# Transposing and loading DMAs taken out of each other's way, residual rows loaded earlier, and the static order of the engines planned anew, in a transformer block of attention and gMLP

## The chip, the cores and the metric

The kernel runs on one core of a Trainium2 chip. Times are device microseconds of that core. Engines: PE is TensorE (matmul), PEld its weight loads, DVE is VectorE, ACT is ScalarE, POOL is GpSimd, SP is SyncE. SP and POOL here mainly issue DMAs, each from one queue worked in order.

## The reference

```python
h  = x + A(layernorm(x))     # x: 2048 x 1024
h2 = h + B(layernorm(h))
# A: q,k,v = x@wqkv; 32 heads of 32; each row attends to 8 rows (0,2,..14 back); then @wo
# B: z = gelu(x@w_in); z1 = left half; z2 = layernorm(right half)
#    g = w_sp @ z2 + b_sp   (w_sp: 2048 x 2048);  return (z1*g) @ w_out
```

## The kernel before

The rows are worked in four chunks of 512. A first phase does q, k, v (`qkv`), attention on DVE, the projection with wo plus residual (`head`), and the two halves of w_in (`b_z2`, `b_z1`). A second phase multiplies by w_sp and w_out. In the first phase a small planner (`Order`) lists every piece of work with an estimated duration, and writes one fixed order for PE, ACT and DVE; engines then only wait on semaphores. DMAs are not in that fixed order.

```python
XRB = 2
o_ = Order({"PE": 22.2, "ACT": 23.3, "DVE": 17.0, "POOL": 17.0},
           {"acc": 3, "L": 1, "prod": 2, "part": 2, "xn": 4})    # start clocks, buffers
X_AT = {1: 18.8, 2: 33.0, 3: 38.0}                               # when x is expected
...
# ln1: four stores of normalised rows, then ONE transposing DMA per chunk
    nc.sync.dma_start_transpose(xnT[c][:], xn_d[c].rearrange("s (a p) -> s a p", p=P))
...
# head: residual rows x ("xr"): two loaded at the start, the others when a buffer is free
    for k in range(min(XRB, TPC)): xr_load(k)
    ...
    V.scalar_tensor_tensor(hb, acc, 1.0, st["xr", il][:], ...)   # h = acc + x
    A.activation(st["xr", il][:], hnc[:, il, :], ACTF.Square, ...)
    if il + XRB < TPC: xr_load(il + XRB)
...
def zload():                                                     # POOL queue, 12 loads
    for i in range((NCH - 1) * TPC):
        dma_w(z2sb[i][:], z2_d[i * P:(i + 1) * P, :])
def wsp0():                                                      # SP queue
    i_ = load_wsp(0)     # transposes 512 x 2048 of w_sp; only order-tied to a z1 store
...
dma_w(wout_a[:], wout_view[:, 0:8, :])                           # POOL queue
dma_w(wout_b[:], wout_view[:, 8:NF, :])
```

Three buffers called `acc` take PE's results. ACT empties them into four buffers (tag "xn"), which SP stores to memory. If SP can't issue a store, ACT soon can't empty, and PE stops.

Of the kernel before, what the change touches and what calls it, by code (L numbers as in the profile page):

```python
# [33 lines left out]
XRB = 2  # L34
# [23 lines left out]
class Order:  # L58

    def __init__(self, clocks, slots):  # L60
        self.ops, self.clock, self.slots, self.table = [], dict(clocks), {k: [0.0] * n for k, n in slots.items()}, None

# [9 lines left out]
    def run(self):  # L72
        left = list(self.ops)
        while left:
            best, cand = None, []
            for o in left:
                if any(d.end is None for d, _ in o.deps):
                    continue
                r = max([d.end + lat for d, lat in o.deps], default=0.0)
                short = False  # L80
                for k in o.take:
                    if self.slots[k]:
                        r = max(r, min(self.slots[k]))
                    else:
                        short = True
                if short:
                    continue
                cand.append((max(r, self.clock.get(o.eng, 0.0)), o))
            assert cand, "nothing can start"
            first = {}  # L90
            for t, o in cand:
                if o.eng not in first or t < first[o.eng]:
                    first[o.eng] = t
            eng = min(first, key=lambda e: first[e])
            mine = [(o.prio, t, o.n, o) for t, o in cand if o.eng == eng and t <= first[eng] + 0.02]
            late = [(o.prio, t, o.n, o) for t, o in cand if o.eng == eng and t > first[eng] + 0.02]
            pick = min(mine, key=lambda x: x[:3])
            for x in sorted(late):
                if x[0] < pick[0] - 0.5 and x[1] < pick[1] + (0.0 if eng == "PE" else 0.3) * pick[3].us:
                    pick = x  # L100
                    break
            _, t, _, o = pick
            if o.table and o.table != self.table:
                t += 1.28
                self.table = o.table
            o.start, o.end = t, t + o.us
            if o.eng in self.clock:
                self.clock[o.eng] = o.end
            for k in o.take:
                self.slots[k].remove(min(self.slots[k]))  # L110
            if o.free:
                self.slots[o.free].append(o.end + 0.1)
            left.remove(o)
        self.ops.sort(key=lambda o: (o.start, o.n))
        for o in self.ops:
            o.fn()

@with_exitstack
def kernel(
# [185 lines left out]
    o_ = Order({"PE": 22.2, "ACT": 23.3, "DVE": 17.0, "POOL": 17.0}, {"acc": 3, "L": 1, "prod": 2, "part": 2, "xn": 4})  # L305
# [6 lines left out]
    X_AT = {1: 18.8, 2: 33.0, 3: 38.0}  # L312
# [3 lines left out]
    def ln1(c):  # L316
# [16 lines left out]
        else:  # L333
# [11 lines left out]
            rs = batch_rstd(("l1", c), lambda: G["xsum", c][:], lambda: G["xsq", c][:], D, "l1", sts, 1.0)  # L345
# [7 lines left out]
        ns = [dma_op(4.0, lambda: None, [n_], free="xn") for n_ in ns]  # L353
        def tr():
            xnT[c] = xtp.tile([P, KT, CH], BF16, name="xnT", tag="xnT")
            nc.sync.dma_start_transpose(xnT[c][:], xn_d[c].rearrange("s (a p) -> s a p", p=P))
        G["xnT", c] = dma_op(8.0, tr, ns + ([G["qkvlast", c - 2]] if c >= 2 else []))
# [7 lines left out]
    def qkv(c):  # L365
        for xi in range(0 if c else 1, 3):
            wv = wsb[xi][:].rearrange("p kt (m dl) -> p kt dl m", dl=DLO)
            for dp in range(DLO // 2):
                key = ("acc", "qkv", c, xi, dp)
                deps = [G.get(("xnT", c))]  # L370
                for j, kh in ((0, 0), (0, 1), (1, 0), (1, 1)):
                    def mm(j=j, kh=kh, dl=2 * dp + j, wv=wv, key=key):
                        if j == 0 and kh == 0:
                            G[key] = new_acc()
                        for kt in range(4 * kh, 4 * kh + 4):
                            G["wdoneins", c] = T.matmul(G[key][:, j, :], wv[:, kt, dl, :], xnT[c][:, kt, :],  # L376
                                                        start=(kt == 0), stop=(kt == KT - 1))
# [19 lines left out]
    def attention(c):  # L397
# [3 lines left out]
        else:  # L401
            def ld(which):
                def f():
# [3 lines left out]
                    dma_w(att_in[c][which][:], qkv_d[which][:, :, lo:(c + 1) * CH])  # L407
                return f
            ev = [G["ev", c, xi, dp] for xi in range(3) for dp in range(4)]
            d_q = dma_op(7.0, ld(0), ev[0:4] + [G["qkdone", c - 1]])  # L410
# [76 lines left out]
        def rec():  # L487
            st["rinv"] = att.tile([P, P], FP32, name="rinv", tag="rinv")
# [4 lines left out]
        for hw in range(2):  # L493
# [7 lines left out]
            for sh in range(2):  # L501
# [10 lines left out]
                pm = add("PE", 0.2, pbm, [wait], prio=1.0, take="acc" if sh else "L", lat=0.2)  # L512
# [7 lines left out]
        for w in range(W_WIN):  # L520
# [15 lines left out]
            else:  # L536
                prev = add("DVE", 2.3, lambda w=w: V.tensor_tensor(oTs[c][:], oTs[c][:], pvs[w][:], op=ALU.add),  # L537
                           [prev, m_], prio=3.0, lat=0.15, free="prod")
        G["avdone", c] = prev

    def batch_rstd(key, sums, sqs, n, pfx, deps, prio, cols=slice(0, TPC), nb=True):
        def a1():
            if cols.start == 0:
# [7 lines left out]
        s2 = add("POOL", 1.05, lambda: nc.gpsimd.tensor_tensor(G[key]["rstd"][:, cols], G[key]["var"][:, cols], nhalf[:, cols], op=ALU.pow),  # L551
                 [s1], lat=POOLLAT)
# [5 lines left out]
    def head(c):  # L558
# [4 lines left out]
        xr0 = dma_op(0.0, lambda: None, [G["attq", c]] if ("attq", c) in G else [])  # L563
        sqd = []
        for il in range(TPC):
            i = c * TPC + il
            deps = [G["avdone", c]]
            for half in range(4):
                def mm(half=half, il=il, i=i):
                    if half == 0:  # L570
                        if il == 0:
# [3 lines left out]
                            for k in range(min(XRB, TPC)):  # L575
                                xr_load(k)
# [5 lines left out]
                def xr_load(k):  # L582
                    st["xr", k] = bp.tile([P, D], BF16, name="xr", tag="xr", bufs=XRB)
                    dma(st["xr", k][:], x2d[(c * TPC + k) * P:(c * TPC + k + 1) * P, :])
# [8 lines left out]
            def hsq(il=il):  # L593
                A.activation(st["xr", il][:], st["hnc"][:, il, :], ACTF.Square, accum_out=st["hsq"][:, il:il + 1])
                if il + XRB < TPC:
                    xr_load(il + XRB)
# [18 lines left out]
        if last:  # L615
            G["close"] = dma_op(0.0, close_, [G["headmm", c]] + [G["z2n", k, il] for k in range(c) for il in range(TPC)])
            tps = []
            for il in range(TPC):
# [6 lines left out]
                t_ = add("PE", 0.45, tpm, [nd[il]], prio=1.0, take="acc")  # L625
# [3 lines left out]
        else:  # L629
            def tr():  # L630
                hnTs[c] = bp.tile([P, TPC, KT, P], BF16, name="hnT", tag="hnT")
                nc.sync.dma_start_transpose(hnTs[c][:].rearrange("p il a s -> p (il a) s"),
                                            st["hnc"][:].rearrange("s il (a p) -> s (il a) p", p=P))
            G["hnT", c] = dma_op(8.0, tr, nd)
# [93 lines left out]

    def load_wo():
        i_ = dma_w(wo_sb[:], A_wo.rearrange("(p dl) n -> p dl n", dl=DLO))  # L730
        tc.add_manual_dep(i_.ins, G["wdoneins", 0].ins.name,
                          mybir.DependencyInfo(mybir.DependencyClass.Sync, mybir.DependencyReason.DATA),
                          reason="load wo behind the first chunk")

    dma_op(8.0, load_wo, [G["wdone", 0, 2]])
# [31 lines left out]
    def zload():  # L767
        for i in range((NCH - 1) * TPC):
            dma_w(z2sb[i][:], z2_d[i * P:(i + 1) * P, :])

    head(NCH - 1)
    dma_op(0.0, zload, [G["hdone", NCH - 1], G["close"]])
# [3 lines left out]
    def wsp0():  # L776
# [3 lines left out]
                          reason="keep the xbar transpose out of the z1 store stream")  # L780

    dma_op(0.0, wsp0, [G["z1ev", NCH - 2], G["close"]])
# [11 lines left out]
    dma_w(wout_a[:], wout_view[:, 0:8, :])  # L794
    dma_w(wout_b[:], wout_view[:, 8:NF, :])
    for c in range(NCH):
        wspT = wspTs[c]
        zg = p2.tile([P, NF, CH], BF16, name="zg", tag="zg")
        for fp in range(NF // 2):
# [3 lines left out]
            for j in range(2):  # L803
                f = 2 * fp + j
                for a in range(NT):
                    T.matmul(acc[:, j, :], z2sb[a][:, f * P:(f + 1) * P], wspT[:, a, :],  # L806
                             start=(a == 0), stop=(a == NT - 1))
# [48 lines left out]
```

## Time and profile before

| | before |
|---|---|
| median, first 4 runs | 733.63 us (732.98 to 734.22) |
| span of the profiled run | 731.48 us |
| PE busy | 720.2 us, 98% |
| first k matmul starts at / span after the last matmul | 23.96 us / 3.33 us |

The first two lines of the profile page of the kernel before, span and engine totals (busy us, share, number of instructions):

```profile
span 731.5 us, 8470 instructions
PE 720.2 (98%) x3453; PEld 365.1 (50%) x3514; DVE 418.1 (57%) x427; ACT 246.5 (34%) x313; POOL 46.8 (6%) x59
```

PE is the bound, and what can be won is its waits. The list of waits of PE in the kernel before (engine, tile, line, releaser: total us, times, longest):

```profile
PE wps L204 <- DVE warm L201: 1.3, 1, 1.3
PE L L453 <- DVE part L437: 1.1, 1, 1.1
PE tp L246 <- DVE xn L235: 0.8, 1, 0.8
PE acc L284 <- ACT xnT L249: 0.5, 1, 0.5
PE tpa L246 <- DVE xn L235: 0.4, 1, 0.4
PE tp L624 <- DVE hb L609: 0.3, 1, 0.3
```

Lines L204, L246 and L284 are the start-up. Only L453 (attention logits, waiting for DVE) and L624 (a transpose on PE, waiting for DVE) lie in the stream.

The list leaves waits out that end inside a matmul's modelled length. A finer reading of the trace compares starts of neighbouring matmuls, which are about 216 ns apart at 512 columns, and calls more than that a stall. One caution: about one matmul record in fifty is missing, and such a hole looks like a stall of 216 ns. The weight loads are recorded completely (3514), so a hole with two weight loads in it is a missing record, and a hole with one is a stall. Read that way, the kernel before has five stalls after 20 us: 0.22 us at 69.3, 0.24 at 214.4, 1.16 at 236.8, 0.23 at 384.4 and 0.47 at 391.8, together 2.32 us.

Why DVE was late at 237 shows in its timeline around the residual addition (start, duration, engine, line, operation, in brackets the idle time before it and what ended it):

```profile
209.53 2.29 DVE L430 TENSOR_TENSOR prod<-qT,kT 128x4096 bf16<-128x4096 bf16 x1
213.48 1.23 DVE L589 SCALAR_TENSOR_TENSOR hb<-acc,xr 128x1024 bf16<-128x1024 f32 x1 [1.67 <-DMA xr<-in_A_x_dram]
```

DVE stood 1.67 us waiting for rows of x that were loaded late, and everything behind it moved.

### The profile page before, as it was taken

The numbers are of one execution on the slowest core, as the hardware profiler recorded it, in microseconds if no ns is written. First come the engines' busy times: TensorE is split into PE (matmuls) and PEld (weight loads), VectorE is DVE, ScalarE is ACT, GpSimd is POOL, SyncE is SP. The second block draws the span as 40 slices with busy tenths as digits, with TensorE's granted clock in tenths as the row PEclk, the third lists the DMA queues.
The fourth block names the chain that finished last, engine by engine and source line by source line (L and its number), as shares of the span: only waits on it lengthen the run. The fifth ranks groups of instructions, "written<-read, shape, count | busy, mean of one in ns | idle before, by whom it ended". The sixth has DMA issues, their size and how long they took to land.

```text
span 731.5 us, 8470 instructions
## 1 busy us (share of the span) xinstructions
PE 720.2 (98%) x3453; PEld 365.1 (50%) x3514; DVE 418.1 (57%) x427; ACT 246.5 (34%) x313; POOL 46.8 (6%) x59
## 2 busy tenths in 40 slices
PE   8999999999999999999999999999999999999998
PEld 3666665666644444444445444444444444444444
DVE  5489999989989999989942102322232223222222
ACT  4396822543338954687634530000000000000000
POOL 0111200100101000100113100000000000000000
PEclk9999999999999999999999999999999999999999
DMA  8976874385682623360239997044115311020002
GB/s 322 353 169 217 229 233 146 119 243 187 215 305 73 231 86 103 102 216 15 108 136 343 248 243 244 30 121 124 58 33 126 116 58 42 25 91 16 1 16 71
DMA packets 113814, 106.30 MB, mean 145 GB/s; under 512 B 67856, under 2 KB 91824, under 8 KB 113648
## 3 DMA queue, kind: packets, MB, share of 16 engines
q1 hardware_dynamic: 105696, 72.82, 33.3%
q0 software_dynamic: 7280, 31.50, 12.7%
q10 hardware_dynamic: 800, 1.44, 0.5%
q8 instruction: 27, 0.44, 0.3%
q14 instruction: 11, 0.09, 0.0%
HBM read 55.09 MB, written 34.93 MB: 123 GB/s over the span
## 4 chain that ended last, share of the span: by engine, by line
PE 89%; DMA 5%; DVE 4%; issue 1%; ACT 1%; SPq 0%; DVEq 0%; ACTq 0%
PE acc L806 26%; PE acc L376 19%; PE acc L825 13%; PE acc L707 12%; PE acc L657 10%; PE acc L580 6%; DVE prod L430 2%; DMA qkv_d<-stg 1%; PE acc L284 1%; DMA xr<-in_A_x_dram 1%; DMA h_d<-hb 1%; DMA xp<-in_A_x_dram 1%; DVE prod L434 1%; DMA wq<-in_A_wqkv_dram 1%; DVE hb L589 1%
## 5 line engine op out<-in xcount | busy, mean ns | idle before, releaser
L806 PE MATMUL acc<-wspT,z2sb 128*128 128x512 bf16 x878 | 193.1, 379 | 0.9
L806 PEld LDWEIGHTS <-z2sb 128*128 128x128 bf16 x896 | 87.7, 98 | 105.7
L809 DVE TENSOR_TENSOR g<-acc,bB 128x1024 bf16<-128x1024 f32 x28 | 34.3, 1224 | 159.5 <-PE acc L806 134.3
L707 PE MATMUL acc<-hnT,win 128*128 128x512 bf16 x448 | 98.7, 379 | 0.1
L657 PE MATMUL acc<-win,hnT 128*128 128x512 bf16 (+1 forms) x500 | 98.0, 352 | 0.7
L430 DVE TENSOR_TENSOR prod<-qT,kT 128x4096 bf16<-128x4096 bf16 x32 | 72.5, 2283 | 8.6 <-DMA xp<-in_A_x_dram 8.6
L657 PEld LDWEIGHTS <-hnT 128*128 128x128 bf16 x512 | 49.8, 98 | 47.7 <-issue 1.1
L825 PEld LDWEIGHTS <-zg 128*128 128x128 bf16 x462 | 45.2, 98 | 51.7
L707 PEld LDWEIGHTS <-win 128*128 128x128 bf16 x448 | 43.4, 98 | 52.6 <-issue 1.9
L531 DVE TENSOR_TENSOR prod<-vT,AB 128x4096 bf16<-128x4096 bf16 x28 | 63.8, 2289 | 1.0
L537 DVE TENSOR_TENSOR oT<-oT,prod 128x4096 bf16<-128x4096 bf16 x28 | 64.0, 2285 | 0.1
L827 DVE TENSOR_TENSOR ot<-acc,hr 128x1024 bf16<-128x1024 f32 (+2 forms) x18 | 19.9, 1106 | 73.1 <-PE acc L825 64.2
L825 PE MATMUL acc<-wout_a,zg 128*128 128x512 bf16 (+1 forms) x260 | 58.0, 372 | 0.3
L376 PE MATMUL acc<-xnT,wk 128*128 128x512 bf16 x251 | 56.2, 379 | 0.3
L376 PE MATMUL acc<-xnT,wv 128*128 128x512 bf16 x250 | 56.1, 380 | 0.3
L580 PE MATMUL acc<-wo_sb,oT 128*128 128x512 bf16 x251 | 55.8, 379 | 0.3
L387 ACT CAST stg<-acc 128x1024 bf16<-128x1024 f32 x36 | 36.2, 1010 | 51.9 <-PE acc L376 42.5
L376 PEld LDWEIGHTS <-wk 128*128 128x128 bf16 x256 | 36.9, 145 | 18.9 <-issue 0.7
L376 PEld LDWEIGHTS <-wv 128*128 128x128 bf16 x256 | 36.7, 145 | 18.8 <-issue 0.9
L825 PE MATMUL acc<-wout_b,zg 128*128 128x512 bf16 (+1 forms) x193 | 43.8, 372 | 0.2
L376 PE MATMUL acc<-xnT,wq 128*128 128x512 bf16 x188 | 42.6, 380 | 0.2
L580 PEld LDWEIGHTS <-oT 128*128 128x128 bf16 x256 | 25.0, 98 | 29.7
(107 smaller groups left out, 525.1 us busy)
## 6 DMA issues: line engine op xcount, KB each, us to landing
qkv_d<-stg SPq DMA_DIRECT2D x36, 256.0 KB, 2.9
z_d<-z1s SPq DMA_DIRECT2D x28, 256.0 KB, 2.6
z1c<-z_d SPq DMA_DIRECT2D x28, 256.0 KB, 2.7
z_d<-u SPq DMA_DIRECT2D x12, 448.0 KB, 2.8
z2sb<-z_d POOLq DMA_DIRECT2D x12, 448.0 KB, 8.1
xr<-in_A_x_dram SPq DMA_DIRECT2D x16, 256.0 KB, 2.6
h_d<-hb SPq DMA_DIRECT2D x16, 256.0 KB, 2.0
win<-in_B_w_in_dram POOLq DMA_DIRECT2D x2, 2048.0 KB, 10.9
```

The source lines that it names most:

```text
L376: G["wdoneins", c] = T.matmul(G[key][:, j, :], wv[:, kt, dl, :], xnT[c][:, kt, :], start=(kt == 0), stop=(kt == KT - 1))
L387: A.copy(stg[:], G[key][:])
L430: V.tensor_tensor(st["prod"][:], qT[:], kT[:, :, o:o + CH], op=ALU.mult)
L531: V.tensor_tensor(pvs[w][:], vT[:, :, o:o + CH], abb, op=ALU.mult)
L537: prev = add("DVE", 2.3, lambda w=w: V.tensor_tensor(oTs[c][:], oTs[c][:], pvs[w][:], op=ALU.add), [prev, m_], prio=3.0, lat=0.15, free="p ...
L580: T.matmul(st["acc", il][:, nh, :], oTs[c][:, dl, il * P:(il + 1) * P], wo_sb[:, dl, nh * CH:(nh + 1) * CH], start=(dl == 0), stop=(dl == ...
L657: T.matmul(accf[:, n0:n1], hnTs[c][:, il, kt, :], wins[hf][:, kt, n0:n1], start=(kt == 0), stop=(kt == KT - 1))
L707: T.matmul(G["accy", c, fp][:, j, :].rearrange("p (a b) -> p a b", a=TPC), wt[:, kt, f0 * P:(f0 + 1) * P], hnTs[c][:, :, kt, :], start=(kt ...
L806: T.matmul(acc[:, j, :], z2sb[a][:, f * P:(f + 1) * P], wspT[:, a, :], start=(a == 0), stop=(a == NT - 1))
L809: V.tensor_tensor(g1[:], acc[:], bB[:, c * CH:(c + 1) * CH].unsqueeze(1).to_broadcast([P, 2, CH]), op=ALU.add)
L825: T.matmul(acc[:, m0 - n0:m1 - n0], zg[:, f, il * P:(il + 1) * P], wt[:, f0, m0:m1], start=(f == 0), stop=(f == NF - 1))
L827: V.tensor_tensor(ot[:, n0:n1], acc[:, 0:n1 - n0], hr[:, n0:n1], op=ALU.add)
```

## The change

Its intent: no PE wait in the first phase. Cut to its core:

```diff
-XRB = 2
+XRB = 4                     # and rinv shares the tag of mx, to make room
-    o_ = Order({"PE": 22.2, "ACT": 23.3, "DVE": 17.0, ...}, {..., "xn": 4})
+    o_ = Order({"PE": 23.4, "ACT": 24.5, "DVE": 18.0, ...}, {...}, {"xn": 4})   # a ring, in order
-    X_AT = {1: 18.8, 2: 33.0, 3: 38.0}
+    X_AT = {1: 18.8, 2: 38.5, 3: 43.5}
     # transposes of xn and h: one for each 128 rows
-            nc.sync.dma_start_transpose(xnT[c][:], ...)
+                nc.sync.dma_start_transpose(xnT[c][:, :, il * P:(il + 1) * P], ...)
     # chunk 1's q load (POOL queue) waits for chunk 2's transposes (SP queue)
+                    if c == 1 and which == 0:
+                        behind(i_, G["xpins", 2, TPC - 1], "load q behind the transposes")
     # residual rows: all four of a chunk, planned in the middle of attention
+        dma_op(0.0, xr_load, [G["avmid", c]])
-                            for k in range(min(XRB, TPC)): xr_load(k)
-                if il + XRB < TPC: xr_load(il + XRB)
     # last PE transpose of h planned 1.1 us later; the two pb matmuls in order
-    t_ = add("PE", 0.45, tpm, [nd[il]], ...)
+    t_ = add("PE", 0.45, tpm, [(nd[il], 1.2 if il == 3 else 0.1)], ...)
     # wo: four pieces, issued about 9 us earlier
+        for j in range(0, DLO, 2):
+            behind(dma_w(wo_sb[:, j:j + 2, :], ...), G["mmins", 0, 2, 1], ...)
     # first w_sp transpose waits for the last z2sb load
+        behind(i_, G["zlast"], "transposing and loading by turns")
     # w_out: loaded after two groups of w_sp matmuls instead of at once
+            if c == 0 and fp == 1:
+                behind(dma_w(wout_a[:], ...), m_, ...); behind(dma_w(wout_b[:], ...), m_, ...)
```

More of the change, by code (lines that the diff above doesn't have):

```diff
@@ L58, with __init__ @@
 class Order:
-    def __init__(self, clocks, slots):
+    def __init__(self, clocks, slots, ring):
         self.ops, self.clock, self.slots, self.table = [], dict(clocks), {k: [0.0] * n for k, n in slots.items()}, None
+        self.ring, self.gone = {k: (n, []) for k, n in ring.items()}, {}
     def add(self, eng, us, fn, deps=(), prio=5.0, lat=0.1, take=None, free=None, table=None):
@@ L81, in run @@
                 for k in o.take:
-                    if self.slots[k]:
+                    if k in self.ring:
+                        n, got = self.ring[k]
+                        if len(got) >= n:
+                            if got[-n] in self.gone:
+                                r = max(r, self.gone[got[-n]])
+                            else:
+                                short = True
+                    elif self.slots[k]:
                         r = max(r, min(self.slots[k]))
@@ L109, in run @@
             for k in o.take:
-                self.slots[k].remove(min(self.slots[k]))
-            if o.free:
+                if k in self.ring:
+                    self.ring[k][1].append(o)
+                else:
+                    self.slots[k].remove(min(self.slots[k]))
+            if o.free in self.ring:
+                self.gone[o.deps[0][0]] = o.end + 0.1
+            elif o.free:
                 self.slots[o.free].append(o.end + 0.1)
@@ L303, in load_win @@
         wins[k] = t
-    o_ = Order({"PE": 22.2, "ACT": 23.3, "DVE": 17.0, "POOL": 17.0}, {"acc": 3, "L": 1, "prod": 2, "part": 2, "xn": 4})
+    o_ = Order({"PE": 23.4, "ACT": 24.5, "DVE": 18.0, "POOL": 18.0}, {"acc": 3, "L": 1, "prod": 2, "part": 2}, {"xn": 4})
     add = o_.add
@@ L344, in ln1 @@
                     sts.append(add("ACT", 1.12, sm, [arrive], prio=7.0 + 0.1 * c, lat=3.0))
-            rs = batch_rstd(("l1", c), lambda: G["xsum", c][:], lambda: G["xsq", c][:], D, "l1", sts, 1.0)
+            rs = G["rsop", c] = batch_rstd(("l1", c), lambda: G["xsum", c][:], lambda: G["xsq", c][:], D, "l1", sts, 1.0)
             for il in range(TPC):
@@ L352, in ln1, with tr @@
                 ns.append(add("ACT", 1.16, nrm, [rs], prio=6.5 + 0.1 * c, take="xn"))
-        ns = [dma_op(4.0, lambda: None, [n_], free="xn") for n_ in ns]
-        def tr():
-            xnT[c] = xtp.tile([P, KT, CH], BF16, name="xnT", tag="xnT")
-            nc.sync.dma_start_transpose(xnT[c][:], xn_d[c].rearrange("s (a p) -> s a p", p=P))
-        G["xnT", c] = dma_op(8.0, tr, ns + ([G["qkvlast", c - 2]] if c >= 2 else []))
+        trs = []
+        for il, n_ in enumerate(ns):
+            def tr(il=il):
+                if il == 0:
+                    xnT[c] = xtp.tile([P, KT, CH], BF16, name="xnT", tag="xnT")
+                G["xpins", c, il] = nc.sync.dma_start_transpose(xnT[c][:, :, il * P:(il + 1) * P],
+                                            xn_d[c][il * P:(il + 1) * P, :].rearrange("s (a p) -> s a p", p=P))
+            kept = dma_op(4.0, lambda: None, [n_], free="xn")
+            trs.append(dma_op(4.0, tr, [kept] + ([G["qkvlast", c - 2]] if c >= 2 else [])))
+        G["xnT", c] = dma_op(2.0, lambda: None, trs)
     seq = [0]
@@ L371, in qkv, with mm @@
                 for j, kh in ((0, 0), (0, 1), (1, 0), (1, 1)):
-                    def mm(j=j, kh=kh, dl=2 * dp + j, wv=wv, key=key):
+                    def mm(j=j, kh=kh, xi=xi, dp=dp, dl=2 * dp + j, wv=wv, key=key):
                         if j == 0 and kh == 0:
@@ L375, in mm @@
                         for kt in range(4 * kh, 4 * kh + 4):
-                            G["wdoneins", c] = T.matmul(G[key][:, j, :], wv[:, kt, dl, :], xnT[c][:, kt, :],
+                            G["mmins", c, xi, dp] = T.matmul(G[key][:, j, :], wv[:, kt, dl, :], xnT[c][:, kt, :],
                                                         start=(kt == 0), stop=(kt == KT - 1))
@@ L406, in f @@
                     lo = c * CH - (HALO if which else 0)
-                    dma_w(att_in[c][which][:], qkv_d[which][:, :, lo:(c + 1) * CH])
+                    i_ = dma_w(att_in[c][which][:], qkv_d[which][:, :, lo:(c + 1) * CH])
+                    if c == 1 and which == 0:
+                        behind(i_, G["xpins", 2, TPC - 1], "load q behind the transposes")
+                        tc.add_manual_dep(i_.ins, G["rstdins", ("l1", 3)].ins.name,
+                                          mybir.DependencyInfo(mybir.DependencyClass.NoSync, mybir.DependencyReason.DATA),
+                                          reason="rstd before the waiting load on POOL's queue")
                 return f
             ev = [G["ev", c, xi, dp] for xi in range(3) for dp in range(4)]
-            d_q = dma_op(7.0, ld(0), ev[0:4] + [G["qkdone", c - 1]])
+            d_q = dma_op(7.0, ld(0), ev[0:4] + [G["qkdone", c - 1]] + ([G["xnT", 2], G["rsop", 3]] if c == 1 else []))
             d_k = dma_op(7.0, ld(1), ev[4:8] + [G["qkdone", c - 1]])
@@ L487, in rec @@
         def rec():
-            st["rinv"] = att.tile([P, P], FP32, name="rinv", tag="rinv")
+            st["rinv"] = att.tile([P, P], FP32, name="rinv", tag="mx")
             V.reciprocal(st["rinv"][:], st["ssum"][:, 0, :])
@@ L511, in pbm @@
                                  start=True, stop=True, tile_position=(32 * sq, 0))
-                pm = add("PE", 0.2, pbm, [wait], prio=1.0, take="acc" if sh else "L", lat=0.2)
+                pm = add("PE", 0.2, pbm, [wait, (pm, 0.0)] if sh else [wait], prio=1.0, take="acc" if sh else "L", lat=0.2)
                 eng = "DVE" if (hw == 0 and sh == 1) else "ACT"
@@ L538, in attention @@
                            [prev, m_], prio=3.0, lat=0.15, free="prod")
+            if w == 2:
+                G["avmid", c] = prev
         G["avdone", c] = prev
@@ L550, in batch_rstd, with a2 @@
         s1 = add("DVE", 0.74, a1, deps, prio=prio)
-        s2 = add("POOL", 1.05, lambda: nc.gpsimd.tensor_tensor(G[key]["rstd"][:, cols], G[key]["var"][:, cols], nhalf[:, cols], op=ALU.pow),
-                 [s1], lat=POOLLAT)
+        def a2():
+            G["rstdins", key] = nc.gpsimd.tensor_tensor(G[key]["rstd"][:, cols], G[key]["var"][:, cols], nhalf[:, cols], op=ALU.pow)
+        s2 = add("POOL", 1.05, a2, [s1], lat=POOLLAT)
         def a3():
@@ L562, in head, with xr_load @@
         prio = 4.0 + c * 0.1
-        xr0 = dma_op(0.0, lambda: None, [G["attq", c]] if ("attq", c) in G else [])
+        def xr_load():
+            for k in range(TPC):
+                st["xr", k] = bp.tile([P, D], BF16, name="xr", tag="xr", bufs=XRB)
+                dma(st["xr", k][:], x2d[(c * TPC + k) * P:(c * TPC + k + 1) * P, :])
+        dma_op(0.0, xr_load, [G["avmid", c]])
         sqd = []
@@ L574, in mm @@
                             st["hnc"] = bp.tile([P, TPC, D], BF16, name="hb", tag="hb", bufs=1)
-                            for k in range(min(XRB, TPC)):
-                                xr_load(k)
                         st["acc", il] = new_acc()
@@ L581, in mm @@
                                      start=(dl == 0), stop=(dl == DLO - 1))
-                def xr_load(k):
-                    st["xr", k] = bp.tile([P, D], BF16, name="xr", tag="xr", bufs=XRB)
-                    dma(st["xr", k][:], x2d[(c * TPC + k) * P:(c * TPC + k + 1) * P, :])
                 m_ = add("PE", 0.8635, mm, deps, prio=prio + il * 1e-2 + half * 1e-3, take="acc" if half == 0 else None)
@@ L594, in hsq @@
                 A.activation(st["xr", il][:], st["hnc"][:, il, :], ACTF.Square, accum_out=st["hsq"][:, il:il + 1])
-                if il + XRB < TPC:
-                    xr_load(il + XRB)
             sqd.append(add("ACT", 1.12, hsq, [r_], prio=3.0, lat=0.25))
@@ L624, in tpm @@
                         T.transpose(st["tp", il][:, a, :], st["hnc"][:, il, a * P:(a + 1) * P], ident)
-                t_ = add("PE", 0.45, tpm, [nd[il]], prio=1.0, take="acc")
+                t_ = add("PE", 0.45, tpm, [(nd[il], 1.2 if il == 3 else 0.1)], prio=1.0, take="acc")
                 tps.append(add("DVE", 0.7, lambda il=il: V.tensor_copy(hnTs[c][:, il], st["tp", il][:]), [t_], prio=0.7, free="acc", lat=0.15))
@@ L629, in head, with tr @@
         else:
-            def tr():
-                hnTs[c] = bp.tile([P, TPC, KT, P], BF16, name="hnT", tag="hnT")
-                nc.sync.dma_start_transpose(hnTs[c][:].rearrange("p il a s -> p (il a) s"),
-                                            st["hnc"][:].rearrange("s il (a p) -> s (il a) p", p=P))
-            G["hnT", c] = dma_op(8.0, tr, nd)
+            trs = []
+            for il in range(TPC):
+                def tr(il=il):
+                    if il == 0:
+                        hnTs[c] = bp.tile([P, TPC, KT, P], BF16, name="hnT", tag="hnT")
+                    nc.sync.dma_start_transpose(hnTs[c][:, il], st["hnc"][:, il, :].rearrange("s (a p) -> s a p", p=P))
+                trs.append(dma_op(4.0, tr, [nd[il]]))
+            G["hnTs", c] = trs
+            G["hnT", c] = dma_op(1.0, lambda: None, trs)
     hnTs, z2sb, pools = {}, {}, {}
@@ L727, with behind @@
     qkv(0)
+    def behind(i_, j_, why):
+        tc.add_manual_dep(i_.ins, j_.ins.name, mybir.DependencyInfo(mybir.DependencyClass.Sync, mybir.DependencyReason.DATA), reason=why)
     def load_wo():
-        i_ = dma_w(wo_sb[:], A_wo.rearrange("(p dl) n -> p dl n", dl=DLO))
-        tc.add_manual_dep(i_.ins, G["wdoneins", 0].ins.name,
-                          mybir.DependencyInfo(mybir.DependencyClass.Sync, mybir.DependencyReason.DATA),
-                          reason="load wo behind the first chunk")
-    dma_op(8.0, load_wo, [G["wdone", 0, 2]])
+        wo_view = A_wo.rearrange("(p dl) n -> p dl n", dl=DLO)
+        for j in range(0, DLO, 2):
+            behind(dma_w(wo_sb[:, j:j + 2, :], wo_view[:, j:j + 2, :]), G["mmins", 0, 2, 1], "load wo behind chunk 1's transposes")
+    dma_op(8.0, load_wo, [G["ev", 0, 2, 1]])
     for c in range(1, NCH):
@@ L768, in zload @@
         for i in range((NCH - 1) * TPC):
-            dma_w(z2sb[i][:], z2_d[i * P:(i + 1) * P, :])
+            G["zlast"] = dma_w(z2sb[i][:], z2_d[i * P:(i + 1) * P, :])
     head(NCH - 1)
-    dma_op(0.0, zload, [G["hdone", NCH - 1], G["close"]])
+    zl = dma_op(0.0, zload, [G["hdone", NCH - 1], G["close"]])
     b_z2(NCH - 1)
@@ L780, in wsp0 @@
                           reason="keep the xbar transpose out of the z1 store stream")
-    dma_op(0.0, wsp0, [G["z1ev", NCH - 2], G["close"]])
+        behind(i_, G["zlast"], "transposing and loading by turns")
+    dma_op(0.0, wsp0, [G["z1ev", NCH - 2], G["close"], zl])
     with tc.manual_schedule(engines=manual):
@@ L793 @@
     dma(bB[:], B_b_sp.unsqueeze(0).to_broadcast([P, S]))
-    dma_w(wout_a[:], wout_view[:, 0:8, :])
-    dma_w(wout_b[:], wout_view[:, 8:NF, :])
     for c in range(NCH):
@@ L805 @@
                 for a in range(NT):
-                    T.matmul(acc[:, j, :], z2sb[a][:, f * P:(f + 1) * P], wspT[:, a, :],
-                             start=(a == 0), stop=(a == NT - 1))
+                    m_ = T.matmul(acc[:, j, :], z2sb[a][:, f * P:(f + 1) * P], wspT[:, a, :],
+                                  start=(a == 0), stop=(a == NT - 1))
+            if c == 0 and fp == 1:
+                behind(dma_w(wout_a[:], wout_view[:, 0:8, :]), m_, "load w_out behind the transposes of w_sp")
+                behind(dma_w(wout_b[:], wout_view[:, 8:NF, :]), m_, "load w_out behind the transposes of w_sp")
             g1 = p2.tile([P, 2, CH], BF16, name="g1", tag="g1")
```

## The prediction

> **What bounds the kernel now.** TensorE. The page's first part gives PE busy 720.2 us of a span of 731.5 (98%), and the row by slices shows full clock throughout. The PE timeline shows where the missing 11.3 us lie: 3.2 us before the stream fills (first 15 us), 3.3 us after the last matmul (728.2 to 731.5: last addition and store), and the rest is many 0.05 us gaps plus very few real waits. The wait list for PE has only two after the start: 1.1 us before the L453 matmuls at 238.3 (waiting for DVE `part`) and 0.3 us before the transposes at 392.5 (waiting for DVE `hb`). Between starts of neighbouring matmuls I find excesses of 1.26 and 0.47 us at these two, and 0.24 us each at 214.4 and 384.4. Together 2.2 us. Everything else on DVE, ACT and the DMA queues is already hidden.
>
> **What the change does.** It adds and removes no compute: the instruction order lists equal PE counts, and the same matmuls. It
> - doubles the xr buffers and loads them earlier. Before, the third xr of chunk 1 landed 7.2 us after its issue (206.2 to 213.4) because w_in loads were running; DVE waited 1.7 us for it. That delay is what shifted DVE's attention work and made PE wait at 214.4 and 238.3.
> - splits the six big DMA transposes (xnT, hnT; 5.8 to 8.8 us to landing) into four each. The 128x8x128 transposes of q show what one costs: 4.3 to 9.2 us to landing, 1.2 to 4.3 us of SP queue time. More queue time in total, but consumers can start at the first part.
> - moves wo, the first q load, w_sp and w_out so that transposes and plain loads alternate. The Trainium skill, "DMA: Bandwidth & Descriptors", section "Issuing engines are not separate DMA queues", says that DMAs from all queues interleave on the same 16 engines; this trace agrees: an h_d store takes 1.96 us alone and 7.1 us beside the z2sb loads, and one w_sp transpose 21.6 us there against 9.4 later.
> - changes the static order of PE, ACT and DVE: buffer use is modelled as a ring, x arrives later (38.5), and PE's start is set 1.2 us later, which comes nearer to the trace (PE ran 1.8 us behind the old plan). The attention matmuls and the last h transpose come later relative to DVE, so PE should not catch DVE up.
>
> **How much is critical.** Transposes, wo, w_sp and w_out were never waited for by PE: xnT landed at 45.3, 78.4 and 105.8 and was used at about 51.6, 96 and 149. Their gain is zero. Only the four PE excesses, 2.2 us, can go. Phase two (after 438 us) has no PE wait, so nothing there.
>
> **Prediction.** 731.8 us, 80% range 729.8 to 734.5. Faster by over 2%: 0.01; within 2%: 0.97; slower by over 2%: 0.02.
>
> **What would show the steps.** PE busy stays 720 us; the waits at 238 and 392 vanish from the PE wait list; DVE's 1.7 us wait for xr vanishes; the first L806 matmul starts near 436 instead of 437.9; w_sp's first transpose lands in about 10 us, at about 414, unused until 436; w_out lands after 452, well before 486.
>
> **What would make it wrong.** Chunk 1's four transposes landing after 51.6 (36.5 plus four issues leaves only about 3 to 5 us of room), then PE stalls there; the q load, waiting on the POOL queue, holding back chunk 3's stores so that ACT cannot evict and PE runs out of accumulators near 90; SP blocked by more transposes, delaying evictions. Each would cost 1 to 5 us. PE records with hidden stalls could make more gain possible, but I see none.

## The result

The changed kernel takes 730.43 us (median of 9 runs, 730.10 to 732.08), against 733.43 us for the kernel before in all its runs so far (13 runs, 732.54 to 736.74). The ratio is 0.9956, 95% interval 0.9943 to 0.9968. A ratio here is the mean time of one kernel's fast runs over that of the other's of the same rounds, so not quite the ratio of the medians. This is faster by 0.4%, "within 2%" as forecast, and inside the forecast range.

Span and engine totals of the changed kernel:

```profile
span 729.1 us, 8507 instructions
PE 719.4 (99%) x3453; PEld 365.0 (50%) x3514; DVE 417.4 (57%) x427; ACT 247.4 (34%) x313; POOL 49.9 (7%) x62
```

The list of waits of PE in the changed kernel:

```profile
PE wps L217 <- DVE warm L214: 1.2, 1, 1.2
PE tpa L259 <- DVE xn L248: 0.6, 1, 0.6
PE tp L259 <- DVE xn L248: 0.5, 1, 0.5
PE acc L297 <- ACT xnT L262: 0.5, 1, 0.5
PE acc L394 <- issue: 0.2, 1, 0.2
```

The first four are start-up. The last, 0.2 us at 84.5, has two weight loads in it: a missing record, no stall. So the stream has none left. DVE's residual addition in the same place, now without a wait:

```profile
210.05 2.29 DVE L453 TENSOR_TENSOR prod<-qT,kT 128x4096 bf16<-128x4096 bf16 x1
212.25 1.22 DVE L614 SCALAR_TENSOR_TENSOR hb<-acc,xr 128x1024 bf16<-128x1024 f32 x1
```

The traces also show how the rows came earlier. Loads of x go out at almost the same times in both kernels around here (206.2, 209.6, 216.0 and 218.3 before; 206.7, 210.1, 214.7 and 217.0 changed), and the first still takes 7.4 us to land beside the w_in loads (7.2 before). But with four buffers these loads carry the rows of the next chunk. The third 128 rows of chunk 1, for which DVE waited until 213.4 before, landed at 135.3 in the changed kernel, loaded as chunk 0 gave its buffers free. The number of buffers and the new place of the loads in the program were not tested apart.

The sum closes. From the first k matmul to the first w_sp matmul (the "stream" below) takes 413.92 us before and 411.61 after: 2.31 us less, which is the 2.32 us of stalls (five after 20 us in the kernel before: 0.22 us at 69.3, 0.24 at 214.4, 1.16 at 236.8, 0.23 at 384.4 and 0.47 at 391.8). From there to the last matmul both take 290.28 us. The start is 0.08 us later, the tail 0.12 us shorter; in all 2.35 us of span. Every build below that shows no stall has a stream of 411.61 us to within 0.02, so its length over 411.61 is a second measure of the stalls.

The medians of all runs differ by 3.0 us, 0.65 more than the spans of the two profiled runs. I come back to it in experiment 9.

### The profile page after: what moved, and what is told of

It reads as the page before. It is cut to its first block, busy times and chain, and to the rows that moved or that the text cites. A ratio compares the mean times of both kernels' runs of the same rounds, so it can differ in the third digit from the quotient of the medians.

```text
span 729.1 us, 8507 instructions
## 1 busy us (share of the span) xinstructions
PE 719.4 (99%) x3453; PEld 365.0 (50%) x3514; DVE 417.4 (57%) x427; ACT 247.4 (34%) x313; POOL 49.9 (7%) x62
## 4 chain that ended last, share of the span: by engine, by line
PE 96%; DMA 1%; DVE 1%; issue 1%; ACT 0%; ACTq 0%; SPq 0%
PE acc L834 26%; PE acc L394 21%; PE acc L734 13%; PE acc L856 13%; PE acc L684 12%; PE acc L608 8%; DMA xp<-in_A_x_dram 1%; PE acc L297 1%; PE L L476 1%; PE pb L533 0%; PE tp L647 0%; DVE attn L521 0%; DVE mx L485 0%; ACT sme L499 0%; PE tpa L259 0%
```

## The experiments

All twelve builds gave correct results. Their edits are shown cut to the lines that matter. The times were taken with the kernel before on the same chip. "Stream" is as defined above, read from each build's trace.

| build | median us (range) | ratio to before | stream us |
|---|---|---|---|
| before | 733.4 to 733.7 | 1 | 413.92 |
| changed | 730.43 (730.10 to 732.08) | 0.9956 | 411.61 |
| xr_only | 731.63 (731.20 to 732.11) | 0.9975 | 413.16 |
| plan_only | 759.10 (753.01 to 771.28) | 1.0332 | 439.05 |
| after_old_xr | 731.55 (731.15 to 732.22) | 0.9973 | 413.34 |
| after_whole_tr | 730.70 (730.27 to 730.98) | 0.9961 | 411.61 |
| after_old_wsp | 730.55 (730.24 to 731.11) | 0.9957 | 411.59 |
| plan_wsp | 732.79 (732.33 to 734.59) | 0.9990 | 413.66 |
| after_old_q | 732.89 (730.54 to 738.39) | 1.0000 | 412.05 |
| lean | 730.62 (730.30 to 730.87) | 0.9956 | 411.61 |
| dma_only | 731.03 (730.58 to 732.83) | 0.9975 | 411.82 |
| lean_no_wsp | 757.95 (730.97 to 765.00) | none | 440.45 |
| after_q6 | 730.96 (729.92 to 735.68) | 0.9976 | 411.61 |
| before_wsp | 733.70 (732.91 to 735.06) | 1.0005 | 416.11 |

My theory (A): late residual rows delay DVE and so PE; the new order removes the rest; the other DMA moves are worth nothing. Rivals: the order alone is the gain (B), or taking transposes and loads apart is (C).

### 1. xr_only: early residual rows alone

```diff
 # on the kernel before
-XRB = 2
+XRB = 4
+        dma_op(0.0, xr_load, [G["avmid", c]])
-                            for k in range(min(XRB, TPC)): xr_load(k)
-                if il + XRB < TPC: xr_load(il + XRB)
```

> The kernel before with only the earlier loading of xr into four buffers (and the shared tag that makes room); PE, DVE and ACT keep the order of before exactly. Of the five PE stalls of before (0.23 us at 69.3, 0.24 at 214.4, 1.16 at 236.8, 0.23 at 384.4, 0.47 at 391.8) theory A (late xr delays DVE) expects those at 214 and 236 to go and the other three to stay: about 1.4 us less, first L806 matmul near 436.5. Rival B (the static order alone is the gain) expects no change, within 0.3 us. Theory C (transposes and loads by turns is the gain) also none.

Measured: 1.9 us faster than before. The stalls at 214 and 237 are gone, as A said, and the one at 392 with them, which A did not say. The early stall grew. The list of waits of PE in this build, without start-up:

```profile
PE acc L376 <- ACT stg L387: 0.9, 1, 0.9
...
PE pb L510 <- ACT AB L515: 0.2, 1, 0.2
```

These two, at 69 and 83 us, are ACT emptying results too late (`stg` is its copy of q, k or v; `pb` spreads attention weights over the partitions, and `AB` is the copy of that). They are the business of experiments 5 and 6. B and C, which expected nothing here, fall as sole causes.

### 2. plan_only: the new order alone

```diff
 # on the kernel before: ring model, start clocks, X_AT, order of pb, latency of the last transpose
-    o_ = Order({"PE": 22.2, ...}, {..., "xn": 4})
+    o_ = Order({"PE": 23.4, ...}, {...}, {"xn": 4})
```

> The kernel before with only the planner's changes (ring model, start clocks, arrival times of x, order of the pb pair, latency of the last h transpose): PE, DVE and ACT get the exact order of the changed kernel, all DMAs stay as before. Theory A: the stalls at 384 and 392 go, 214 stays (DVE still waits 1.7 us for xr), 236 goes or shrinks as PE comes there later; 69 stays since wo still loads beside the stores: 0.7 to 1.9 us less. Rival B: all five go, 2.2 to 2.5 us less, as the full change. Theory C: nothing gained.

Nobody expected this: 25.6 us slower than before by the medians of all runs, and 24.4 by the means of those that count as fast (five of six; the slowest, 771.28, counts as slow). The list of waits of PE in this build, without start-up:

```profile
PE acc L819 <- ACT z1s L726: 24.1, 1, 24.1
PE pb L523 <- ACT AB L528: 1.6, 1, 1.6
PE L L466 <- DVE part L450: 1.5, 1, 1.5
```

Take the two small ones first. The wait for `part`, which the new order was said to avoid by letting PE come later, is still there and longer (1.5 us against 1.1); the order does not remove it. The four small stalls of before (69, 214, 384, 392) are gone, and a new one came, of 1.6 us at 83.

The big one is a chain: PE waits for ACT, ACT for a z1 store, the store for SP. The timeline of the SP queue of plan_only around it (start and duration of the issue):

```profile
390.95 56.38 SPq L738 DMA_TRANSPOSE wspT<-in_B_w_sp_dram  x1
447.42 8.23 SPq L727 DMA_DIRECT2D z_d<-z1s  x3
```

The same two lines of the kernel before and of the changed kernel, first before:

```profile
390.29 19.53 SPq L725 DMA_TRANSPOSE wspT<-in_B_w_sp_dram  x1
418.40 7.27 SPq L714 DMA_DIRECT2D z_d<-z1s  x3
```

and changed:

```profile
403.44 7.63 SPq L752 DMA_TRANSPOSE wspT<-in_B_w_sp_dram  x1
416.18 7.27 SPq L741 DMA_DIRECT2D z_d<-z1s  x3
```

The transpose of the first quarter of w_sp holds the SP queue for 56 us in plan_only, 20 us before, 8 us in the changed kernel. Stores queue behind it. Before, the queue came free 8.6 us ahead of the first store that ACT made behind it, and nobody noticed. ACT in plan_only, with its wait:

```profile
428.12 1.02 ACT L726 ACTIVATE z1s<-acc 128x1024 bf16<-128x1024 f32 x1 [2.43 <-PE acc L720]
461.44 2.85 ACT L726 ACTIVATE z1s<-acc 128x1024 bf16<-128x1024 f32 x3 [32.29 <-DMA z_d<-z1s]
```

After its idle time PE was also slow: its second to eleventh w_sp matmuls started about 427 ns after one another, and from the twelfth on 216 again. The Trainium skill, "TensorE: Matmul & The Clock Gate", section "What's actually happening", says that an idle array drops to half its clock and needs sustained work to get it back; this trace agrees, with a granted clock of 0.74 in the stretch of 427 to 460 us and double the distance afterwards. It cost about 2 us more (292.4 us from the first w_sp matmul to the end, against 290.3).

### 3. after_old_xr: the changed kernel without early residual rows

```diff
 # on the changed kernel
-XRB = 4
+XRB = 2     # and the old loads
```

> The changed kernel with the old loading of xr (two buffers, the third and fourth after the square). Theory A: DVE waits about 1.7 us for xr again near 212, PE stalls again by 0.24 us near 214 and perhaps near 238, so 0.2 to 1.4 us slower than the changed kernel. Rival B: within 0.2 us of the changed kernel.

Measured: 1.1 us slower than the changed kernel by medians, stalls of 1.38 us at 238 and 0.36 at 88. The first line of its list of waits of PE that is not start-up:

```profile
PE L L476 <- DVE part L460: 1.3, 1, 1.3
```

DVE in this build waits for the rows again, beside the new order:

```profile
214.15 1.22 DVE L614 SCALAR_TENSOR_TENSOR hb<-acc,xr 128x1024 bf16<-128x1024 f32 x1 [1.92 <-DMA xr<-in_A_x_dram]
```

With experiment 1, this shows early xr to be what removes the largest stall, in either order. B falls a second time. The wait of DVE did not bring the small stall at 214 back, perhaps because PE's new order has room there; this was not tested.

### 4. after_whole_tr: the six transposes whole again

```diff
 # on the changed kernel
-                nc.sync.dma_start_transpose(xnT[c][:, :, il * P:(il + 1) * P], ...)
+            nc.sync.dma_start_transpose(xnT[c][:], ...)        # and likewise hnT
```

> The changed kernel with the six transposes whole again, order on PE, DVE and ACT the same. Theories A and B: no PE stall comes back, within 0.3 us of the changed kernel. Theory C: some or all of the 2.3 us come back.

Measured: no stall, stream 411.61, ratio 0.9961 against 0.9956. Splitting gains nothing that these runs can see.

### 5. after_old_q: the q load not kept behind the transposes

```diff
 # on the changed kernel
-                        behind(i_, G["xpins", 2, TPC - 1], "load q behind the transposes")
```

> The changed kernel, but the q load of chunk 1 is not kept behind chunk 2's transposes. If the stall near 83 in plan_only (1.6 us) comes from that load running beside the transpose (the transpose held SP from 70.9 to 79.6 there and stores queued behind it), a stall of 0.3 to 1.6 us comes back between 80 and 90. If splitting the transposes is what removed it, nothing comes back (within 0.3 us of the changed kernel).

Measured: in the profiled run a stall of 0.45 us came back at 83 us (PE `pb` waiting for ACT `AB`, as in plan_only), within what was expected:

```profile
PE pb L528 <- ACT AB L533: 0.4, 1, 0.4
```

The times of all six runs say more: three lie at 730.5 to 730.9, three at 734.9 to 738.4. In the changed kernel itself, of its own nine runs, the worst is 732.1. They were run at other times. So the q load beside the transposes seems to cost nothing on some runs and 4 to 8 us on others. Six runs are few, and no trace fell on a slow one; where the 4 to 8 us are spent is open.

### 6. dma_only: all DMA parts, the old order

```diff
 # on the changed kernel: the planner of before
-    o_ = Order({"PE": 23.4, ...}, {...}, {"xn": 4})
+    o_ = Order({"PE": 22.2, ...}, {..., "xn": 4})
```

> The changed kernel with the planner of before: PE, DVE and ACT keep exactly the order of the kernel before, all DMA parts of the change are in (early xr, split transposes, wo, q, w_sp and w_out moved). Theory F (the DMA parts carry the gain and the new order is only one way to have no stall): at most the 0.23 us stall near 384 stays, within 0.5 us of the changed kernel. Theory G (the order matters too, since ACT's statistics of chunks 2 and 3 are planned before x has landed): a stall of 0.5 to 1.5 us stays near 69 to 83, so 0.7 to 1.7 us slower than the changed kernel.

Measured: by the trace, F holds. One stall of 0.24 us is left, at 383, and the stalls at 69 and 83 that xr_only had are gone. So of the 2.31 us, the DMA parts carry 2.10 in that old order. By the times it is less clear: three runs at 730.6 to 731.0, two at 732.6 and 732.8, which makes the ratio 0.9975. Either the old order meets late DMAs in some runs and the traced one was a good one, or this is chance. Open.

Which DMA part removes the stall at 69 in the old order was not isolated. xr does not (it stays in xr_only), the w_sp wait does not (it stays in experiment 9); left are wo, q and splitting. In the trace of before, a q store issued at 56.3 took 9.05 us to land beside the wo load, against 2.1 alone, and ACT waited 5.7 us for it. In the trace of dma_only, where wo had landed by 56.8 instead of 63.4, the same store took 2.4 us and ACT did not wait. No transpose and no q load was in flight in either trace from 56 to 60, so this points to wo and not to q or splitting; no build changes wo alone, so an experiment for it is missing.

### 7. plan_wsp and after_old_wsp: the w_sp wait alone, and all but it

```diff
 # plan_wsp: plan_only with        (after_old_wsp: the changed kernel without)
+        behind(i_, G["zlast"], "transposing and loading by turns")
```

> The kernel before with the planner's changes and the wait of the first w_sp transpose for the last z2sb load, nothing else. Theory D: the 24 us stall of plan_only goes, the transpose lands in about 10 us, and the two stalls of plan_only near 83 (1.6 us) and 239 (1.6 us) stay: about 734 us, no faster than before. Rival E: a stall of 10 us or more stays because w_out is still loaded early.

> The changed kernel, but the first w_sp transpose no longer waits for the last z2sb load (it may run in the midst of the loads, as before); the order on every engine is that of the changed kernel. Theory D (a transpose in the midst of the z2sb loads slows both, and in the plan's order this fills the SP queue until ACT and PE stop): the transpose takes 20 to 70 us to land, and if over about 45 us, PE stalls before the first L834 matmul, up to 24 us, as in plan_only. Rival E (the 24 us in plan_only came from w_out being loaded at the same time, which the changed kernel still has moved away): the transpose lands in about 20 us and nothing is lost, within 0.5 us of the changed kernel.

Measured: plan_wsp loses the 24 us stall; the transpose lands in 12 us; the two small stalls stay (0.66 us at 83, 1.39 at 239), and it is as fast as before:

```profile
PE L L466 <- DVE part L450: 1.3, 1, 1.3
...
PE pb L523 <- ACT AB L528: 0.6, 1, 0.6
```

So the disaster needs the transpose in the midst of the loads. But after_old_wsp, where it is in their midst as well, loses nothing. The line on landing from the view of the w_sp transposes' source line (shortest, median and longest of the four), first of the kernel before:

```profile
DMA to landing us min/median/max: 9.4/10.4/21.6
```

The same line of plan_only:

```profile
DMA to landing us min/median/max: 9.5/11.8/69.4
```

The same line of after_old_wsp:

```profile
DMA to landing us min/median/max: 9.9/10.9/42.9
```

And of the changed kernel:

```profile
DMA to landing us min/median/max: 9.6/10.2/10.9
```

In after_old_wsp the transpose took 43 us, D's figure, not E's 20; SP was free again at 427.3, three waiting z1 stores went out at once, and PE did not stall. In plan_only it took 26.5 us more. There the last z2sb load landed 44.5 us after the transpose was issued, against 36.6 in after_old_wsp; from then on the transpose needed another 24.8 us with w_out loading beside it (issued at 427.7 and 429.7, landed by 459.9), against 6.3 without. So the w_out loads can account for up to 18.5 of the 26.5 us. The other 8 are slower z2sb loads, and that delay was there before w_out was issued: the fifth of them landed 36 us after the transpose's issue, against 24. Why is open.

D and E were each half right. With the new order, the loss came in the two builds that have neither the w_sp wait nor the w_out move (plan_only, and lean_no_wsp in experiment 8), and in none that has one of them. No build differs in the w_out move alone: after_old_wsp and lean_no_wsp differ also in wo and in splitting, whose transfers end some 70 us before the transpose starts.

Why the new order alone ran into it: when the transpose was issued, 9 of the 12 z2sb loads were already out in the kernel before and in xr_only, but only 4 in plan_only, after_old_wsp and lean_no_wsp. From the first of these loads to the transpose passed 7.3 us before (383.0 to 390.3) and 4.3 in plan_only (386.7 to 391.0): in the new order SP has one z1 store to issue ahead of the transpose there, and had two before.

What the two kinds of DMA do to each other shows in the trace's packet records, summed by queue (not a view of the page):

```
                     z2sb loads (POOL queue)        w_sp transpose (SP queue)
changed, 396-400     407 GB/s, packets of 5.6 KB    -
changed, 408-412     -                              290 GB/s, packets of 256 B
plan_only, 398-402   195 GB/s, 137 packets          14 GB/s, 223 packets
plan_only, 410-414    39 GB/s,  27 packets          21 GB/s, 325 packets
```

The Trainium skill, "DMA: Bandwidth & Descriptors", section "Queues, rings and completion order", says that a DMA engine takes turns between its queues packet by packet. The 398-402 row fits only roughly: 1.6 transpose packets of 256 B for each load packet of 5.7 KB, where turns would give one, if the packets of the trace are those of the page. With such sizes the transpose gets a small share of the bytes. The 410-414 row does not follow from turns: it has 12 transpose packets for each load packet, and both transfers were slow, 60 GB/s together, where either alone does over 200. The records add that a transpose packet took 18 ns on average where the transpose was alone, but 136 and 216 ns in the two rows beside the loads, while a load packet took 223 to 253 ns in all of them. (Records overlap, so part of this may be waiting.) Why is open. The view by windows shows it for the whole stretch in plan_only (us, busy time of PE, PEld, DVE, ACT, POOL, granted clock, DMA share, GB/s):

```profile
391.00:427.00 36.00, 36.00 (x196) 18.33 (x195) 2.76 (x8) 18.29 (x27) 4.65 (x9) 1.00 1.19 157
427.00:460.00 33.00, 11.45 (x54) 4.99 (x51) 2.96 (x5) 1.02 (x1) 3.22 (x3) 0.74 1.22 171
```

and in the changed kernel for the loads alone and then the transpose alone:

```profile
384.00:403.40 19.40, 19.30 (x116) 10.36 (x117) 5.31 (x13) 10.05 (x16) 7.87 (x14) 1.00 0.85 312
403.40:413.10 9.70, 9.65 (x53) 5.14 (x53) 0.42 (x3) 5.94 (x11) 0.00 (x0) 1.00 0.98 216
```

The DMA share (next to last) is higher in plan_only; only the bytes (last) tell that its DMA engines were occupied without moving much.

### 8. lean and lean_no_wsp: only the parts that seemed to matter

```diff
 # lean: on the kernel before: planner, early xr, q behind the transposes, w_sp behind z2sb
 #       (transposes whole, wo and w_out as before)
 # lean_no_wsp: lean without
-        behind(i_, G["zlast"], "transposing and loading by turns")
```

> The kernel before with four of the parts only: the planner's changes, the early xr loads, the q load behind the transposes, and the w_sp transpose behind the z2sb loads. Transposes stay whole, wo and w_out are loaded as before. If these four are what matters, no PE stall over 0.1 us after 20 us, and the time is that of the changed kernel within 0.5 us (730.0 to 731.2). If the moves of wo or w_out, or the splitting, matter too, one or more stalls of 0.2 us or more come back.

> lean without the wait of the first w_sp transpose for the z2sb loads. If the 24 us stall needs two things together (a transpose in the midst of the z2sb loads, and w_out loaded on top of it), it comes back here: the transpose takes over 50 us to land and the time is 745 to 770 us. If something else in plan_only made it, this kernel stays at 730 to 732 us.

Measured: lean has no stall and the changed kernel's time, with the narrowest range of all (730.30 to 730.87). In the new order, splitting the transposes and moving wo and w_out gain nothing on top. lean_no_wsp took 755 to 765 us in five runs of six and 731 in the sixth; its trace shows PE waiting for ACT z1s as in plan_only:

```profile
PE acc L827 <- ACT z1s L731: 28.7, 1, 28.7
```

Because of the one quick run the five count as slow; plan_only, where all six runs were over 19 us slower than before and five of them count as fast, carries the point. The quick run shows that the collision is a matter of timing and need not happen every time.

### 9. before_wsp: the w_sp wait on the kernel before

```diff
 # on the kernel before
+        behind(i_, G["zlast"], "transposing and loading by turns")
```

> The kernel before with only the wait of the first w_sp transpose for the last z2sb load; order unchanged on all engines. The prediction put its gain at zero: the transpose lands in about 10 us instead of 21.6, near 414, and the time is within 0.4 us of before, with the same PE stalls. If the slow transpose was costing before anything, it is faster by more.

Measured: ratio 1.0005; the transpose lands in at most 10.9 us instead of 21.6; nothing is gained. But the profiled run showed 4.5 us of stalls, the five of before with two of them much longer: 1.9 us at 69, 0.7 at 216. The first of them in the list of waits of PE:

```profile
PE acc L376 <- ACT stg L387: 1.7, 1, 1.7
```

Its time is no worse than that of before, and the added wait acts only near 390 us, so these stalls belong to the old order and vary from run to run.

They do not explain the 0.65 us by which the gain in the medians exceeds that in the two traces. The profiled run of before took 733.28 us, 0.15 under the median of its runs; that of the changed kernel took 730.94, 0.51 over its own. So most of the excess is that the traced run of the changed kernel was one of its slower ones. Traces without a stall agree in the stream to 0.02 us, but over all traces with this start-up the first k matmul starts between 23.47 and 24.04 us, and 24.04 is the changed kernel's. The start-up is thus the likely place; this is argued, not shown.

### 10. after_q6: an attempt to go further

```diff
 # on the changed kernel, in the start-up
-                if kt == QSPLIT and i + 1 < TPC:
+                if kt == QSPLIT + (i == 1) and i + 1 < TPC:
```

> The changed kernel, with the PE transposes of the third x tile put one K step later inside the second tile's q matmuls. In the changed kernel's profile PE waits 0.64 us at 14.9 for that tile's normalisation, with two K steps of matmuls (0.43 us each) still unissued behind it. Moving one ahead should shorten the wait by up to 0.43 us: 729.9 to 730.4 us. If ACT's copy of the transposes then comes too late, the gain shrinks to nothing.

Measured: in the trace the start-up wait at 14.9 us is gone, and the first k matmul starts at 23.30 us, against 24.04 in the changed kernel and 23.47 to 24.04 in all other traces; the span, 728.4 us, is the shortest. The times do not show a gain: three runs at 729.9 to 730.2, but also 731.8, 732.5 and 735.7. It is not shown to beat the changed kernel.

## Why the prediction was right or wrong

- **PE bounds, and only its waits can go: right.** The stream lost exactly its stalls. I had counted 2.2 us; there were 2.3: the stall at 69 (0.22) was not in my count, and the largest was put 0.1 too high.
- **The size: a little too small.** 731.8 was said, 1.8 under the 733.63 of the first runs, although 2.2 were counted; the prediction does not say why. Measured were 730.43 and a gain of 3.0. In the traces the loss of stalls was 2.3 us. Most of the rest is that the traced run of the changed kernel was 0.5 us slower than the median of its runs (experiment 9). The forecast range, 729.8 to 734.5, holds the time of the kernel before as well, so that the hit in time alone would show little; what carries the judgement is that the stalls went where the prediction said.
- **Early xr removes the stalls at 214 and 237: right**, shown from both sides (experiments 1 and 3).
- **"The attention matmuls ... come later relative to DVE, so PE should not catch DVE up": wrong.** With the new order and the old xr loads PE still waited 1.3 to 1.5 us there. In plan_only the order removes the four small stalls, and a new one of 1.6 us is at 83 (xr_only, in the old order, has 0.3 there); the largest goes only with xr.
- **"Transposes, wo, w_sp and w_out ... Their gain is zero": right for each step taken from before, wrong as a judgement of the change.** Splitting was zero (experiment 4), the w_sp wait was zero on before (9). But the w_sp wait, or the w_out move, is what makes the new order possible: with neither, plan_only lost 25.6 us. And wo, q or splitting removed early stalls in the old order, by the one trace of that build (6). I had asked whether PE waits for these transfers now, and not what a new order would do to when they start.
- **The risks named** (chunk 1's transposes landing too late; q holding up stores) did not come true in the changed kernel: the last of the four transposes landed at 47.7, with PE there at about 51.6. The risk that did exist, an SP queue blocked by a transpose, I named in general but put at 1 to 5 us; where the guards are missing, plan_only shows 24.
- **Details:** the first w_sp matmul started at 435.65 (said: near 436), the w_sp transpose landed at 413.1 (said: about 414), w_out at 465.3, well ahead of its use at 484.

## What to carry to other kernels

When PE is 98% busy, add up its stalls from the starts of neighbouring matmuls, with the weight loads to tell a missing record from a stall; that sum is the whole prize, and it should close afterwards. A guard that gains nothing on the old kernel can still be what the new one stands on, so take a change apart from both ends: each part alone on the old version, and the new version without each part. A queue that is worked in order turns one slow transfer into a stall of everything behind it, so see how much slack each long transfer has before moving what runs beside it.

## What the Trainium skill lacked or had wrong

- "Advanced Engine Details and Errata", section "X-Bar Transpose (TRN2)", says "TRN2 transpose DMAs are as fast as regular DMAs". Here a w_sp transpose (2 MB, alone) took 9.65 us to land, 217 GB/s over that time, at best 290 GB/s in a 4 us stretch, where the plain z2sb loads reached 407.
- No page has what a transpose and plain loads from another queue do to each other's speed. "DMA: Bandwidth & Descriptors", "Rules for kernel authors", says in a row about corrupted results that a transpose next to ordinary DMAs needs nothing. Results were correct in all runs, but one transpose took 21.6 us beside three late loads, 43 beside eight, and 69 where w_out came as well, and total traffic fell to 157 GB/s in that last case, against 312 and 216 with the two one after the other.
- The same page, "Queues, rings and completion order", explains turns by packet, but none of the pages I read says what they mean for a transpose beside loads. In plan_only, with packets of 256 B and 5.7 KB, the two got 14 and 195 GB/s in one stretch, and 21 and 39 in another.
